# Splitting the halves of exchanged weight blocks over two DMA queues in a lightning-attention and tanh-shrink kernel

## The chip, the cores and the metric

The kernel runs on one core of one Trainium2 chip. The metric is the device time of one execution in microseconds (us), the median of several. A core has five engines that run side by side, each in its own order: TensorE (PE) for matrix products, VectorE (DVE) and ScalarE (ACT) for elementwise work, GpSimd (POOL) and SyncE (SP). Data moves between the chip's memory and the core's buffers by DMA. A DMA is issued as an instruction on SP, ACT or POOL, in that engine's order. The profile shows an engine's issuing as SPq, ACTq or POOLq.

## What is computed

```python
for b in range(nb):                      # blocks of 64 positions, 4 batches, 8 heads of width 64
    sl = slice(b * block, (b + 1) * block)
    qb, kb, vb = (q[:, :, sl], k[:, :, sl], v[:, :, sl])
    intra = np.einsum('bhic,bhjc->bhij', qb, kb) * Dmask[None]
    intra = np.einsum('bhij,bhjd->bhid', intra, vb)
    inter = np.einsum('bhid,bhde->bhie', qb * lam_pow[None], kv_state)
    out[:, :, sl] = intra + inter
    kb_dec = kb * rev_pow[None]
    kv_state = lam_block[None, :, None, None] * kv_state + np.einsum('bhsd,bhse->bhde', kb_dec, vb)
...
x = out.transpose(0, 2, 1, 3).reshape(3072, 512)
h = x @ w_in                             # 512 x 2048
g = h - np.tanh(h)
return g @ w_out                         # 2048 x 512
```

q, k, v are float32 with 4 batches, 8 heads, 768 positions and width 64. The weights w_in and w_out arrive with 64 bits to an element, and the kernel rounds them to float32 itself.

## The kernel before

The sequence is cut into six groups of 128 positions of all four batches (512 rows). Each group passes through the attention and then through the two products with the weights. From the second group on, the products use a Strassen scheme with seven products instead of eight, two levels deep in part. Group 0 is computed plainly, because its time is also the time in which the weights are loaded and rounded: `up_plain` (L740) makes `h`, its tanh and `g`, and `down_plain` (L763) the product with w_out.

The weights come in blocks. `blocks` (L190) lists 16 blocks of w_in, unit u (0 to 3, 512 columns of w_in each) by i (0 to 3, 128 rows each), and then 16 of w_out. This text writes (u,i) for a block of w_in. One block is a tile `raw64` of 128 partitions with 512 numbers of 8 bytes, 512 KB. `load_block` (L195) issues its DMA: for w_out on POOL (L198), for i = 0 and 1 of w_in as one DMA of 128 partitions on SP (L200). For i = 2 and 3, the exchanged blocks, it issues two DMAs of 64 partitions and 256 KB each (L203), one behind the other on SP: the upper and the lower 64 rows change places, because the attention's output has its heads in that order there.

`load_weights(n)` (L205) issues the loads of the first n blocks. There are four `raw64` buffers (`WAHEAD`, L68), so the load of a block waits until the block four places before it has been read. `weights(n)` (L215) rounds the first n blocks, each by `round_block` (L252), and keeps the loads four blocks ahead. Rounding a block is two ACT instructions (`Abs` at L261, here "abs", and a copy of the low words into a buffer `r` at L264, of which there are two), and then four on DVE (L265, L267, L269, L271). L269 and L264 are the last to read the raw block, and L271 finishes the float32 block `w`.

At the start (L277 to L284) SP gets, in this order: q, k, v of batches 0 and 1, q and k of batch 2, blocks (0,0) and (0,1), q and k of batch 3, block (0,2) in two halves, v of batches 2 and 3, and block (0,3) in two halves. Then follow the other blocks. `tied` (L118) keeps the instructions that it is given in the order in which they are written; the loads of w_in are tied. All else may be moved by the scheduler of the framework, which lays down a fixed order for each engine when the program is built. The sequence of group 0 is written out by hand from L784 to L818: attention steps of two batches at a time (`att_transpose`, `att_decay`, `att_scores`, `att_state`, `att_out`), with steps of `up_plain(0, ...)` (the generator `half`) and calls of `weights` between them. `up_plain(u, cs)` goes through the blocks i = 0 to 3 for the output banks `cs`, of which there are four (11, 21, 12, 22), each with eight matmul rows in the profile to a pair of banks and block, or four for one bank. When the last block of a bank is done, ACT takes the tanh (`th`, L757) and DVE subtracts it (`g`, L758).

Of the kernel before, what the change touches and what calls it, by code (L numbers as in the profile page):

```python
# [23 lines left out]
def kernel(  # L24
# [32 lines left out]
    nc = tc.nc  # L57
# [60 lines left out]
    def tied(yes, op):  # L118
        return tc.keep_in_program_order(op) if yes else op
# [69 lines left out]
    w_in_u = moe_w_in.rearrange("k (a n) -> k a n", a=2)  # L189
    blocks = [("in", u, i) for u in range(NU) for i in range(KI)] + [("out", kt, a) for kt in range(KH)  # L190
                                                                    for a in range(2)]
    ready = {"loaded": 0, "done": 0}
    wraw, pair = {}, {}

    def load_block(eng, dst, kind, n, m, first=False):  # L195

        if kind == "out":
            eng.dma_start(out=dst, in_=moe_w_out[ts(m * KH + n, 128), :].rearrange("k (a n) -> k a n", a=2))  # L198
        elif m < 2:
            tied(first, eng.dma_start(out=dst, in_=w_in_u[ts(m, 128), :, ts(n, 256)]))  # L200
        else:
            for j in range(2):
                tied(first, eng.dma_start(out=dst[ts(1 - j, 64)], in_=w_in_u[ts(2 * m + j, 64), :, ts(n, 256)]))  # L203

    def load_weights(n):  # L205

        while ready["loaded"] < min(n, len(blocks)):
            if moe_w_in.dtype != F32:
                raw64 = stage.tile([128, 2, 256], I64, name="raw64", tag="raw64", bufs=WAHEAD)
                block = blocks[ready["loaded"]]  # L210
                load_block(nc.sync if block[0] == "in" else nc.gpsimd, raw64, *block, block[0] == "in")
                wraw[ready["loaded"]] = raw64
            ready["loaded"] += 1

    def weights(n):  # L215

        while ready["done"] < min(n, len(blocks)):
            at_ = ready["done"]
            load_weights(at_ + WAHEAD)
            kind, n_, m = blocks[at_]  # L220
            if kind == "out" and m == 0:
                pair[n_] = wst.tile([128, 8, 256], F32, name="wt", tag="w")
            w = w1[n_][:, m] if kind == "in" else pair[n_][:, 2 * m:2 * m + 2]
            if at_ in wraw:
                round_block(w, wraw.pop(at_), at_ < 2 * KI)
            else:
                load_block(nc.gpsimd, w, kind, n_, m)
            ready["done"] += 1
# [44 lines left out]
    def bank(name, tag, bufs):  # L273
        return psum.tile([128, 512], F32, name=name, tag=tag, bufs=bufs)
# [45 lines left out]
    def att_scores(g, bs):  # L320
        for b in bs:
            qt, kt, _ = tr[g, b]

            sp = [bank("sp", "att", 4).rearrange("s (p i) -> s p i", p=NP) for _ in range(2)]
            for p in range(NP):
                for j in range(2):
                    tied(g == 0, nc.tensor.matmul(out=sp[j][:, p, :], lhsT=kt[ts(j, 64), p, :],  # L327
                                                  rhs=qt[ts(j, 64), p, :], start=True, stop=True))
            ss = work.tile([128, 2, NP, BLK], F32, name="ss", tag="ss")
            for j in range(2):  # L330
                tied(g == 0, nc.vector.tensor_tensor(ss[:, j], sp[j], mask[:, j], op=AL.mult))  # L331
            sc[g, b] = ss
# [26 lines left out]
    def att_out(g, bs):  # L359
        half = bs[0] // 2  # L360
        xt[g, half] = xpool.tile([128, KI, HB], F32, name=f"xt{half}", tag=f"xt{half}")

        ops = [bank("op", "att", 4).rearrange("d (p b s) -> d p b s", p=2, b=2) for _ in range(2)]

        def dst(n, p, j):
            return ops[p // 2][ts(j if p < 2 else 1 - j, 64), p % 2, n, :]


        if g > 0:
            for n, b in enumerate(bs):  # L370
                for p in (0, 1):
                    for j in range(2):
                        r = ts(j, 64)
                        for pp in (p, p + 2):
                            nc.tensor.matmul(out=dst(n, pp, j), lhsT=state[r, b, pp, :], rhs=tr[g, b][2][r, pp, :],  # L375
                                             start=n == 0 and p == 0, stop=False, skip_group_check=True)
        for n, b in enumerate(bs):
            ss, vn = sc.pop((g, b)), raw[g, b]["v"]
            for p in range(NP):
                for j in range(2):  # L380
                    tied(g == 0, nc.tensor.matmul(out=dst(n, p, j), lhsT=vn[:, 2 * p + j, :], rhs=ss[:, j, p, :],  # L381
                                                  start=g == 0 and n == 0 and p % 2 == 0,
                                                  stop=n == 1 and p % 2 == 1, skip_group_check=True))
        for x in range(2):
            tied(g == 0, nc.scalar.activation(
                xt[g, half][:, 2 * x:2 * x + 2, :].rearrange("d p (b s) -> d p b s", b=2), ops[x], AF.Copy))
# [353 lines left out]
    def up_plain(u, cs):  # L740

        hm = {}
        for c in cs:
            a, t = divmod(c - 11, 10)
            hm[c] = bank("h", ("ya", "yb", "z", "w")[2 * t + a], 1).rearrange("q (m c) -> q m c", m=2)
        for i in range(KI):
            for c in cs:
                a, t = divmod(c - 11, 10)
                for m in range(2):
                    tied(u == 0, nc.tensor.matmul(  # L750
                        out=hm[c][:, m, :], lhsT=w1[u][:, i, a, ts(m, 128)], rhs=xt[0, t][:, i, :],
                        start=m == 0 and i == 0, stop=i == KI - 1, skip_group_check=True))
                if (i, c) != (KI - 1, cs[-1]):
                    yield
        for c in cs:
            th = work.tile([128, 2, HB], F32, name="th", tag="th")
            nc.scalar.activation(th, hm[c], AF.Tanh)  # L757
            nc.vector.tensor_tensor(hidden(0, c)[:, u], hm[c], th, op=AL.subtract)  # L758
        yield
# [29 lines left out]
    half = up_plain(0, (11, 21))  # L789
    att_transpose(0, (2,))  # L790
    att_decay(0, 2)
    weights(1)
    att_out(0, (0, 1))
    att_scores(0, (2,))
    next(half)
    weights(2)
# [139 lines left out]
```

## Time and profile before

| | |
|---|---|
| median of 3 runs | 673.6 us |
| lowest, highest | 673.12, 675.31 us |
| the profiled execution | 674.1 us |
| its span, first to last instruction | 672.3 us |
| TensorE clock granted | 1.000 |
| PE rows in the profile | 4824 |
| DMA queue of SP (q1) | 133,536 packets, 31.50 MB |
| DMA queue of POOL (q0) | 28,976 packets, 96.49 MB |

A row of the profile's groups, waits or timeline names the line of the kernel, the engine and the tiles, written as output <- inputs. A wait is put down to what came last by the profile. In the timeline the columns are the start, the time taken, engine and line, the operation, the shapes and the number of instructions that were merged, with the idle time before them in brackets. In the chain of waits the columns are the start, the time taken, and what it was.

The stage that the change lies in is the first 85 us. Its busy times by stretch, with the number of instructions:

```profile
core 0: us, PE busy (x) PEld busy (x) DVE busy (x) ACT busy (x) POOL busy (x), PEclk, DMA share, GB/s
...
15.00:20.00 5.00, 3.98 (x50) 3.26 (x46) 4.09 (x9) 3.48 (x7) 0.00 (x0) 1.00 1.09 236
20.00:25.00 5.00, 4.20 (x32) 3.48 (x32) 3.87 (x7) 2.44 (x4) 0.00 (x0) 1.00 1.04 206
25.00:32.00 7.00, 5.87 (x77) 4.75 (x76) 4.70 (x10) 3.95 (x8) 0.00 (x0) 1.00 0.91 236
32.00:40.00 8.00, 8.00 (x39) 7.04 (x38) 7.59 (x16) 5.75 (x10) 0.00 (x0) 1.00 0.68 203
40.00:50.00 10.00, 10.00 (x48) 8.81 (x47) 9.93 (x20) 6.80 (x13) 0.00 (x0) 1.00 0.75 211
```

In the first three of these stretches PE is idle for part of the time; from 32 us on it is busy throughout. POOL does nothing there. DVE is busy for 9.93 of the 10 us from 40 to 50.

### The profile page before, as it was taken

How to read it: one execution, taken by the hardware profiler on the slowest of the kernel's cores; microseconds unless marked ns; L12 is line 12 of the kernel's file. 1: busy time of each engine (PE TensorE's matmuls, PEld its weight loads, DVE VectorE, ACT ScalarE, POOL GpSimd, SP SyncE). 2: the span in 40 equal slices, each digit the busy share in tenths (PEclk: the TensorE clock that was granted, in tenths of full speed). 3: DMA queues.
4: the chain of work that ended last, by engine and by line, in shares of the span. 5: the costliest groups of instructions: out<-in, count | busy, mean ns of one | idle time of the engine just before them, and what ended most of it. 6: DMA issues, size and time to landing. Idle time of an engine off the chain costs nothing.

```text
span 672.3 us, 12869 instructions
## 1 busy us (share of the span) xinstructions
PE 661.7 (98%) x4824; PEld 576.3 (86%) x4824; DVE 481.3 (72%) x872; ACT 194.8 (29%) x373; POOL 200.5 (30%) x345
## 2 busy tenths in 40 slices
PE   8899999999999999999999999999999999999998
PEld 7688855558888999988999988899988899988997
DVE  4797867993887772499895379888358977357743
ACT  4564433423331111332112243112333112234110
POOL 0001424217332424244345201254300245400351
PEclk9999999999999999999999999999999999999999
DMA  9979799869855978587898632698730677610495
GB/s 209 222 205 236 238 268 255 290 147 271 249 148 139 243 191 210 127 239 236 228 285 253 176 80 58 150 292 255 225 73 13 160 236 220 217 35 1 126 289 164
DMA packets 162717, 128.80 MB, mean 192 GB/s; under 512 B 133856, under 2 KB 135008, under 8 KB 162656
## 3 DMA queue, kind: packets, MB, share of 16 engines
q0 software_dynamic: 28976, 96.49, 45.4%
q1 hardware_dynamic: 133536, 31.50, 23.6%
q8 instruction: 38, 0.62, 0.4%
q14 instruction: 23, 0.19, 0.1%
q10 hardware_dynamic: 144, 0.00, 0.0%
HBM read 103.55 MB, written 24.38 MB: 190 GB/s over the span
## 4 chain that ended last, share of the span: by engine, by line
PE 86%; issue 8%; DMA 2%; SPq 1%; POOL 1%; DVE 0%; ACT 0%; POOLq 0%; DVEq 0%; ACTq 0%
PE y L433 13%; PE y L695 11%; PE op L771 8%; PE z L433 8%; PE zw L695 8%; PE h L750 7%; PE w L642 4%; PE y L642 4%; PE y L517 4%; PE sp L327 3%; PE plain L642 3%; PE op L381 3%; PE z L517 2%; PE op L375 2%; PE kv L349 1%
## 5 line engine op out<-in xcount | busy, mean ns | idle before, releaser
L607 POOL DMA_DIRECT2D wb<-fine x147 | 79.4, 541 | 114.7 <-PE y L695 48.2
L610 POOL DMA_DIRECT2D wb<-factors x56 | 30.3, 543 | 155.2 <-PE y L642 97.3
L441 ACT ACTIVATE th<-g 128x512 f32<-128x512 f32 x76 | 47.6, 630 | 98.3 <-DVE g L446 33.2
L433 PE MATMUL y<-xt,w 128*128 128x256 f32 x320 | 74.0, 380 | 0.0
L433 PEld LDWEIGHTS y<-xt,w 128*128 128x128 f32 x320 | 59.9, 190 | 9.0 <-ACT g L521 0.9
L442 DVE TENSOR_TENSOR g<-g,th 128x512 f32<-128x512 f32 x76 | 51.9, 688 | 18.2 <-ACT th L441 18.1
L698 ACT ACTIVATE q<-y 128x128 f32<-128x128 f32 x84 | 23.3, 278 | 130.1 <-PE y L695 126.5
L750 PE MATMUL h<-xt,w 128*128 128x256 f32 x256 | 56.5, 381 | 2.0 <-DVE w L271 2.0
L771 PE MATMUL op<-wt,g 128*128 128x512 f32 x128 | 56.5, 595 | 0.0
L750 PEld LDWEIGHTS h<-xt,w 128*128 128x128 f32 x256 | 48.2, 190 | 9.2 <-DVE w L271 1.4
L695 PE MATMUL y<-wb,g 128*128 128x128 f32 x384 | 51.2, 278 | 0.0
L771 PEld LDWEIGHTS op<-wt,g 128*128 128x128 f32 x128 | 23.8, 190 | 27.7 <-issue 26.5
L695 PEld LDWEIGHTS y<-wb,g 128*128 128x128 f32 x384 | 46.4, 192 | 1.2 <-issue 0.3
L433 PE MATMUL z<-tt,ws 128*128 128x256 f32 x160 | 38.0, 380 | 0.0
L433 PE MATMUL z<-xt,ws 128*128 128x256 f32 x160 | 37.9, 380 | 0.0
L433 PE MATMUL y<-tt,ws 128*128 128x256 f32 x160 | 37.8, 379 | 0.0
L642 PE MATMUL y<-wb,g 128*128 128x256 f32 x160 | 35.6, 379 | 0.5 <-PE y L433 0.5
L198 POOL DMA_DIRECT2D raw<-in_moe_w_out_dram x16 | 8.9, 555 | 90.8 <-DVE g L758 52.3
L642 PE MATMUL w<-wb,g 128*128 128x256 f32 x160 | 35.8, 382 | 0.0
L331 DVE TENSOR_TENSOR ss<-sp,mask 128x512 f32<-128x512 f32 x48 | 30.9, 682 | 6.0 <-PE sp L327 6.0
L642 PEld LDWEIGHTS y<-wb,g 128*128 128x128 f32 x160 | 30.3, 190 | 5.0 <-PE y L433 0.9
L433 PEld LDWEIGHTS z<-xt,ws 128*128 128x128 f32 x160 | 30.3, 190 | 4.3 <-ACT g L449 0.2
(171 smaller groups left out, 1301.2 us busy)
## 6 DMA issues: line engine op xcount, KB each, us to landing
wb<-fine POOLq DMA_DIRECT2D x147, 256.0 KB, 3.9
wb<-factors POOLq DMA_DIRECT2D x68, 256.0 KB, 4.2
raw<-in_moe_w_out_dram POOLq DMA_DIRECT2D x16, 512.0 KB, 5.2
v_nat<-in_v_dram SPq DMA_DIRECT2D x24, 256.0 KB, 5.4
factors<-wt POOLq DMA_DIRECT2D x8, 768.0 KB, 5.0
wb<-fine_in POOLq DMA_DIRECT2D x24, 256.0 KB, 4.1
k_nat<-in_k_dram SPq DMA_DIRECT2D x20, 256.0 KB, 5.0
raw<-in_moe_w_in_dram SPq DMA_DIRECT2D x8, 512.0 KB, 5.9
```

Of the source, the lines that this page charges most:

```text
L331: tied(g == 0, nc.vector.tensor_tensor(ss[:, j], sp[j], mask[:, j], op=AL.mult))
L433: nc.tensor.matmul(out=t[:, m, :], lhsT=wt[:, kt, ts(m, 128)], rhs=x[:, kt, :], start=first and m == 0 and kt == 0, stop=kt == 1, skip_gro ...
L441: nc.scalar.activation(th, src, AF.Tanh)
L442: nc.vector.tensor_tensor(dst(c), src, th, op=AL.subtract)
L517: nc.tensor.matmul(out=dst[:, ts(u, 128)], lhsT=a, rhs=b, start=x in (1, 2, 5) and u == 0, stop=True, skip_group_check=True)
L607: nc.gpsimd.dma_start(out=t.rearrange("p m c -> p (m c)"), in_=fine[TWICE.index(n_), SUB.index(x_)].rearrange("p u c -> p (u c)"))
L610: nc.gpsimd.dma_start(out=t, in_=factors[XAT[FACT[n_][1]]][:, 2 * x_:2 * x_ + 2, :])
L642: nc.tensor.matmul(out=t[:, m, :], lhsT=a[:, u, kt, ts(m, 128)], rhs=wb[:, kt, :], start=first and u == 0 and m == 0 and kt == 0, stop=u = ...
L695: nc.tensor.matmul(out=dst, lhsT=a[:, u, :], rhs=wb[:, ts(u, 128)], start=x in (1, 2) and u == 0, stop=u == NU - 1, skip_group_check=True)
L698: nc.scalar.activation(keep, dst, AF.Copy)
L750: tied(u == 0, nc.tensor.matmul(out=hm[c][:, m, :], lhsT=w1[u][:, i, a, ts(m, 128)], rhs=xt[0, t][:, i, :], start=m == 0 and i == 0, stop= ...
L771: nc.tensor.matmul(out=obank[b], lhsT=g, rhs=wt[:, 2 * a:2 * a + 2, :], start=kt == 0 and a == 0, stop=kt == KH - 1 and a == 1)
```

## The change

The two DMAs of an exchanged block go to two queues. The lower half of the tile (rows 2m+1, `half(eng, 1, first)`) stays on SP, tied as before. The upper half goes to another queue. For unit 0 its issue is put into a list `deferred`, which is worked off on ACT, tied, after `att_out(0, (0, 1))`. For units 1 to 3 it is issued on POOL, not tied. The w_out blocks and the blocks of i = 0 and 1 are loaded as before.

```diff
     ready = {"loaded": 0, "done": 0}
-    wraw, pair = {}, {}
+    wraw, pair, deferred = {}, {}, []
 
     def load_block(eng, dst, kind, n, m, first=False):
...
         elif m < 2:
             tied(first, eng.dma_start(out=dst, in_=w_in_u[ts(m, 128), :, ts(n, 256)]))
         else:
-            for j in range(2):
-                tied(first, eng.dma_start(out=dst[ts(1 - j, 64)], in_=w_in_u[ts(2 * m + j, 64), :, ts(n, 256)]))
+
+            def half(queue, j, yes):
+                tied(yes, queue.dma_start(out=dst[ts(1 - j, 64)], in_=w_in_u[ts(2 * m + j, 64), :, ts(n, 256)]))
+
+            half(eng, 1, first)
+            if n == 0:
+                deferred.append((half, nc.scalar, 0, True))
+            else:
+                half(nc.gpsimd if first else eng, 0, False)
...
     att_decay(0, 2)
     weights(1)
     att_out(0, (0, 1))
+    for fn, *args in deferred:
+        fn(*args)
     att_scores(0, (2,))
     next(half)
     weights(2)
```

## The prediction

> **What bounds the kernel now.** I read the page's busy table first, then the waits of TensorE (PE), then the chain of work over the first 75 us, and last the timelines of SP, ScalarE (ACT), VectorE (DVE) and PE there, because all that the change touches is issued before 52 us.
>
> ```profile
> PE 661.7 (98%) x4824; PEld 576.3 (86%) x4824; DVE 481.3 (72%) x872; ACT 194.8 (29%) x373; POOL 200.5 (30%) x345
> ...
> PE h L750 <- DVE w L271: 2.0, 2, 1.0
> PE tp L311 <- ACT qt L313: 0.8, 1, 0.8
> PE kv L349 <- DMA v_nat<-in_v_dram: 0.2, 1, 0.2
> ```
>
> PE is busy 98% of the span, so time can be won only in its few idle stretches, while every stall that is added to PE's order comes on top. The waits of PE under 35 us are 1.0 us at 18.44 and 0.96 us at 31.41 (the two of the first line), 0.8 us at 20.80 and 0.2 us at 26.09. The first is block (0,0), loaded before anything that moves. The second ends in this chain:
>
> ```profile
> 13.43 3.06 SPq L203
> ...
> 19.27 2.89 SPq L203
> ...
> 22.20 5.92 DMA raw<-in_moe_w_in_dram
> ...
> 28.20 0.68 ACT w L261
> ...
> 30.66 0.70 DVE w L271
> ...
> 31.41 43.65 PE h L750 x201
> ```
>
> "SPq" is the SP queue busy with issuing: an issue that takes 0.6 us [...] took 3.06 and 2.89 us at the first halves of blocks (0,2) and (0,3). The last half of (0,3) then lands 5.92 us after its issue, at 28.12; ACT and DVE round the block by 31.36, and PE starts on it 0.96 us late. From 31.41 PE runs without a gap to 81.58 and beyond:
>
> ```profile
> 31.41 50.34 PE L750 MATMUL h<-xt,w 128*128 128x256 f32 x232 [0.96 <-DVE w L271]
> ```
>
> That is the cover of units 1 to 3. It is thinnest at block (1,3). One block for one output bank is four rows of this group, 4 x 50.34/232 = 0.868 us. After (0,3) come 2 + 8 such pieces of unit 0 and three of unit 1, so PE reaches (1,3) at 31.41 + 13 x 0.868 = 42.7. DVE finishes it at 40.78 + 0.69 = 41.47, ahead of both `g` subtractions:
>
> ```profile
> 37.80 0.66 ACT L261 ACTIVATE w<-raw 128x512 f32<-128x512 f32 x1
> 39.54 0.60 ACT L757 ACTIVATE th<-h 128x512 f32<-128x512 f32 x1 [1.08 <-PE h L750]
> 40.03 0.68 ACT L264 ACTIVATE r<-raw 128x512 int32<-128x512 uint32 x1
> 40.61 0.59 ACT L757 ACTIVATE th<-h 128x512 f32<-128x512 f32 x1
> 41.42 0.68 ACT L261 ACTIVATE w<-raw 128x512 f32<-128x512 f32 x1 [0.23 <-DMA raw<-in_moe_w_in_dram]
> ...
> 40.78 0.69 DVE L271 CUSTOM_DVE_ANT_0 w<-w,r 128x1024 uint16<-128x1024 uint16 x1
> 41.38 1.28 DVE L758 TENSOR_TENSOR g<-h,th 128x512 f32<-128x512 f32 x2
> ```
>
> The slack of (1,3) is thus 1.2 us; ACT's rows at 37.80 and 41.42 are the blocks (2,0) and (2,1), each taken as it lands.
>
> [...] the halves of (2,3) land at 45.12 and 46.40, 256 KB in 1.28 us (205 GB/s), those of (2,2) 1.08 us apart (243 GB/s), and block (0,1) of 512 KB lands 1.53 us after (0,0) (343 GB/s). [...] The trace shows only ACT's one issue of 4 KB: 0.42 us.
>
> **Part 1, unit 0: two halves leave SP and go to ACT.** SP loses two issues; (0,2) and (0,3) keep their lower halves there. ACT gets two issues behind the `xt` copies, that is at 17.37. At SP's unhindered 0.55 to 0.60 us they take 1.15 us. ACT is idle from 18.48 to 20.08 (1.60 us, waiting for PE's transposes), and DVE takes the one thing behind them, the rounding of (0,1), only at 19.41; delayed by 1.15 us, its `Abs` ends at about 19.1. So the issues are hidden, with 0.45 us to spare. Below nothing isn't possible for ACT; above, the bound is the rival B.
>
> What it gains: [...] v for batches 2 and 3 moves up by one half, and the last half of (0,3) by one half of its own and one of (0,2). Against this ACT's two halves (landing, by SP's 4.8 to 5.5 us, at 22.5 to 23.5) share the engines. If all serialize[...], the sum of bytes before (0,3) is the same and it lands at 28.1, while v for batch 3 lands one half (1.1 us) later, at 27.05: PE's products with it, then `op` and (0,2), end at 31.5, and (0,3) starts where it starts now. Gain 0. If they overlap[...], (0,3) lands up to 1.1 us earlier, and all 0.96 us of the gap goes; what is late next is v (25.95) and PE's own work before it. (0,2) has room either way: rounded at 27.05, used at 28.45. I take 0.4 us.
>
> **Part 2, units 1 to 3: six halves go from SP to POOL.** POOL is idle until 53.61, and waits there for the same slot as SP does. Six issues of 0.53 us cost PE nothing; its w_out loads stay behind them in block order. A load of 512 KB from POOL lands 4.3 to 4.5 us after an issue on a quiet queue, a block from SP 4.8 to 5.2. So pairs land together, about 1 us earlier than now. That is worth nothing, since PE has no gap here.
>
> **Part 3, what moves with it.** PE's order is the same. But the built order of ACT and DVE in unit 1 changes (lines of the kernel before):
>
> ```
> ACT before: abs(1,3) r(1,3) abs(2,0) th  r(2,0) th      abs(2,1)
> ACT after:  abs(1,3) abs(2,0) r(1,3) r(2,0) th abs(2,1) th
> DVE before: L269(1,2) L271(1,2) .. L269(1,3) L265(2,0) L271(1,3) g g
> DVE after:  L265(2,0) L269(1,2) L267(2,0) L271(1,2) .. g L269(1,3) g L271(1,3)
> ```
>
> Rounding (1,2) now stands behind (2,0), and finishing (1,3) behind the second `g`, whose tanh stands behind abs(2,1). Both blocks are still waited for. With the landings of today (37.77 and 41.40; SP issues them when (1,0) and (1,1) are used up, at 32.95 and 36.25, as now) and these rows' durations:
> - by (2,0): abs 37.80, DVE L265 38.52, L269(1,2) 38.85, L267 39.45, L271(1,2) 39.79 to 40.48; it frees the `r` buffer, so r(2,0) 40.53, th 41.10, abs(2,1) 41.60, th 42.18, g 42.81, L271(1,3) 43.41 to 44.10.
> - by (2,1): landed 41.40, abs 41.42, th 42.0, g 42.6, L271(1,3) 43.2 to 43.9.
> So PE reaches (1,3) at 44.15, not 42.7: 1.4 us lost. [...] it rises by each us that they land later. Behind it (2,3) has 4.5 us of slack, (3,2) and (3,3) 4.4 and 3.7; their new orders use up 2 to 3 us, so nothing more is lost. After 85 us the orders agree.
>
> **Sum.** The stall is 1.4, the start gives 0.4 back and shifts everything with it: +1.0 us. The profiled execution took 674.1 us (span 672.3 and 1.8 around it), 0.5 over the median of 673.6. So 675.1 on its scale and 674.6 on the median's, +0.15%. A measurement tells about 0.3%, 2.0 us, from no change.
>
> **The cases.**
> - A, the forecast, 0.60: 674.6, own range 673.6 to 675.4 (gain 0.96 and stall 1.0, to gain 0 and stall 1.8).
> - B, slower, 0.15: ACT's issues are held up. [...] they wait while SP pushes v [...], and take SP's 1.43 to 3.06 us each. For: SP's issues in just that stretch[...]. Place: ACT's `qt` of batch 3 at 20.08. Two issues are 2.9 to 6.1 us; less 1.6 of idle time and the 0.96 at 31.41, 0.3 to 3.5 are lost, in the middle 1.9. With the stall of 1.4: +3.3, 676.9. It decides from some 1.6 us an issue.
> - C, 0.15: the second queue slows the blocks that (1,3) now waits for. One block of unit 3 took 6.11 us to land; at that, (2,1) lands at 42.36 and (1,3) starts at 44.9, +2.2 with no gain at the start: 675.8, the edge of what can be told.
> - D, 0.10: the blocks land early enough that the new order costs nothing, and the whole gap goes: -1.0, 672.6. The 0.8 us at 20.80 (k for batch 3, landed 20.66, issued before anything moves) would have to go too for -1.8.
> That the change does nothing is A with both terms near 0. Faster by over 0.3% needs more idle time than the touched stretch has: 0.05. Slower gets most of B, two thirds of C and a little of A: 0.29. Within: 0.66. The range 672.8 to 677.0 leaves out part of B.
>
> **What would show it.** Right: the gap before PE's (0,3) shrinks from 0.96; a new PE wait `h L750 <- DVE w L271` of 1 to 2 us near 43; ACT's issues take under 0.7 us each and `qt` stays near 20.1; no new PE gap from 45 to 85. Wrong: no wait near 43, ACT's `qt` past 20.5, v for batch 3 after 27, or gaps after 100 us that differ from today's.

## The result and the profile after

The changed kernel takes 677.06 us (22 runs, 674.47 to 679.62) beside 673.59 us of the kernel before in the same comparison (22 runs, 672.21 to 675.31). The ratio is 1.0049 with an interval of 1.0038 to 1.0060: slower by 2.6 to 4.0 us, where +1.0 had been forecast. The profiled execution took 677.29 us (span 675.5), 3.2 more than that of the kernel before. From `load_weights` on, the lines of the changed kernel stand 8 lower down in the file than those of the kernel before.

Waits of PE over the whole span (who waited for what: total us, times, longest):

```profile
PE h L758 <- DVE w L279: 2.8, 3, 1.4
PE kv L357 <- DMA v_nat<-in_v_dram: 1.9, 1, 1.9
...
PE z L441 <- DVE g L472: 0.9, 1, 0.9
PE y L703 <- DMA wb<-fine: 0.8, 1, 0.8
```

The first two are those of before, one more in number and much longer for `v_nat` (it was 0.2). The third is new. PE's busy time is the same (662.0 us, it was 661.7), so nearly all of the loss is waiting. Its timeline shows where:

```profile
20.00 0.60 PE L319 MATMUL tp<-ident,k_nat 128*128 128x128 f32 x4
...
27.00 0.69 PE L357 MATMUL kv<-v_nat,k_nat 128*64 128x64 f32 x16 [1.90 <-DMA v_nat<-in_v_dram]
...
32.02 11.49 PE L758 MATMUL h<-xt,w 128*128 128x256 f32 x52 [0.66 <-DVE w L279]
44.24 2.00 PE L758 MATMUL h<-xt,w 128*128 128x256 f32 x8 [0.74 <-DVE w L279]
...
179.34 2.00 PE L441 MATMUL z<-xt,ws 128*128 128x256 f32 x8 [0.89 <-DVE g L472]
```

Put instruction by instruction beside the trace of before, PE's lateness grows in these steps: the transposes at 20.80 came 0.80 us earlier, v's products at 26.09 came 0.91 late, block (0,3) is 0.61 late (32.02 for 31.41), block (1,3) 1.51 (44.24 for 42.73), the product `z` 2.67 (179.34 for 176.67), and the end about 3.2. That is +0.6 at the start, +0.9 at (1,3), +1.2 near 179 us, and about +0.5 in single waits for `wb<-fine` after 440 us, net of one of 0.96 us that only the kernel before had (at 643.95).

The step at (1,3) is the one that had been worked out, as DVE's timeline shows:

```profile
41.70 0.69 DVE L766 TENSOR_TENSOR g<-h,th 128x512 f32<-128x512 f32 x1
42.31 0.68 DVE L277 SCALAR_TENSOR_TENSOR w<-raw,w 128x512 uint32<-128x512 uint32 x1
42.91 0.68 DVE L766 TENSOR_TENSOR g<-h,th 128x512 f32<-128x512 f32 x1
43.51 1.28 DVE L279 CUSTOM_DVE_ANT_0 w<-w,r 128x1024 uint16<-128x1024 uint16 x2
```

The finishing operation of (1,3) (L279) starts at 43.51, behind both `g`; PE starts at 44.24. The forecast had 43.41 and 44.15. The block itself wasn't late: its second half had landed at 36.54, and ACT was done with it at 38.99.

ACT's and SP's timelines at the start:

```profile
16.18 0.69 ACTq L205 DMA_DIRECT2D raw<-in_moe_w_in_dram  x1
...
16.90 1.64 ACTq L205 DMA_DIRECT2D raw<-in_moe_w_in_dram  x1
...
18.59 0.68 ACT L269 ACTIVATE w<-raw 128x512 f32<-128x512 f32 x1 [1.05 <-issue]
...
20.26 0.60 ACT L321 ACTIVATE qt<-tp 128x512 f32<-128x512 f32 x1 [0.42 <-PE tp L319]
```

```profile
13.20 3.28 SPq L205 DMA_DIRECT2D raw<-in_moe_w_in_dram  x1
16.54 2.08 SPq L130 DMA_DIRECT2D v_nat<-in_v_dram  x2
18.66 2.55 SPq L205 DMA_DIRECT2D raw<-in_moe_w_in_dram  x1
```

ACT's second issue took 1.64 us while SP was issuing v (2.08 us from 16.54), yet the idle time behind it hid this: `qt` starts at 20.26, 0.18 later than before. SP, with one half less to issue ahead of v, still took 3.28 and 2.55 us for the halves that it kept. What counts is the order of the landings: SP's half of (0,2) at 20.46, ACT's 22.23, v of batch 2 at 23.79, ACT's half of (0,3) 25.46, v of batch 3 at 26.87 (before 25.95), SP's half of (0,3) 28.71 (before 28.12). 256 KB land every 1.4 to 1.8 us, the first five alternately from SP's and from ACT's queue. So not only v is late. From the landing of k for batch 3 to that of the last half of (0,3), these six transfers took 9.4 us, and 7.5 before. PE's last wait ahead of (0,3), 0.66 us at 32.02, is for that block.

### The profile page after: what moved, and what is told of

Same layout as the page of the kernel before. It is cut to its first block, busy times and chain, and to the rows that moved or that the text cites. A ratio compares the mean times of both kernels' runs of the same rounds, so it can differ in the third digit from the quotient of the medians.

```text
span 675.5 us, 12875 instructions
## 1 busy us (share of the span) xinstructions
PE 662.0 (98%) x4824; PEld 577.1 (85%) x4824; DVE 481.5 (71%) x872; ACT 194.8 (29%) x373; POOL 203.7 (30%) x351
## 4 chain that ended last, share of the span: by engine, by line
PE 74%; issue 9%; DMA 7%; DVE 4%; POOL 2%; SPq 2%; ACT 1%; POOLq 0%; DVEq 0%; ACTq 0%
PE y L441 11%; PE y L703 10%; PE z L441 7%; PE zw L703 7%; PE h L758 6%; PE op L779 5%; PE w L650 4%; PE y L650 4%; PE y L525 4%; PE plain L650 3%; DMA raw<-in_moe_w_in_dram 3%; PE sp L335 3%; PE op L389 2%; PE z L525 2%; SPq L142 2%
## 5 line engine op out<-in xcount | busy, mean ns | idle before, releaser
L650 PEld LDWEIGHTS w<-wb,g 128*128 128x128 f32 x160 | 30.1, 190 | 4.3
```

Source lines behind the costliest of these rows:

```text
L650: nc.tensor.matmul(out=t[:, m, :], lhsT=a[:, u, kt, ts(m, 128)], rhs=wb[:, kt, :], start=first and u == 0 and m == 0 and kt == 0, stop=u = ...
```

## The experiments

Two explanations of the steps after 85 us stood against each other. T1: PE, late by 1.5 us, meets a crowded stretch of DMAs worse than before. T2: the six POOL transfers change something fixed in POOL's later stream. Every kernel was timed in turn with the kernel before on the same chip, 5 to 22 times, and the ratios are to that. The last four columns are from the one profiled execution: PE's start at (0,3), its wait at (1,3), POOL's idle time ahead of a transfer near 151 us, and PE's wait at `z`, a product of a later group, near 178 us. The transfer carries sums of w_out blocks (pair kt 7) to `factors`, a buffer in the chip's memory; the recorded texts call it the factors load. Lines stand 9 lower than in the kernel before in e1, e2, e9 and e12, 8 in e8, 12 in e10 and 13 in e11.

| kernel | median us | ratio, interval | (0,3) | (1,3) | POOL | near 178 |
|---|---|---|---|---|---|---|
| before | 673.6 | 1 | 31.41 | none | 9.31 | none |
| changed | 677.06 | 1.0049 (1.0038 to 1.0060) | 32.02 | 0.74 | 10.36 | 0.89 |
| e1 ACT alone | 675.46 | 1.0038 (1.0025 to 1.0051) | 31.93 | none | 9.32 | none |
| e2 POOL alone | 675.57 | 1.0041 (1.0027 to 1.0054) | 30.79 | 1.07 | 10.36 | 0.85 |
| e3 six small | 676.28 | 1.0039 (1.0027 to 1.0050) | 31.45 | none | 10.36 | 0.77 |
| e4 PE late | 675.63 | 1.0031 (1.0019 to 1.0043) | 30.45 | none | 9.31 | none |
| e5 unchanged | 673.71 | 1.0007 (1.0000 to 1.0013) | 30.53 | none | 9.32 | none |
| e6 memsets | 674.38 | 1.0021 (1.0013 to 1.0029) | 31.09 | none | 9.32 | none |
| e7 eight small | 675.66 | 1.0030 (1.0020 to 1.0040) | 31.19 | none | 9.30 | none |
| e8 tied | 679.73 | 1.0089 (1.0071 to 1.0107) | 34.06 | none | 10.36 | 1.08 |
| e9 units 2, 3 | 674.21 | 1.0015 (1.0006 to 1.0024) | 31.23 | none | 10.31 | 0.47 |
| e10 changed + two | 676.12 | 1.0037 (1.0025 to 1.0049) | 31.49 | 0.78 | 9.30 | none |
| e11 e9 + four | 674.62 | 1.0020 (1.0013 to 1.0028) | 31.67 | none | 9.30 | 0.24 |
| e12 ACT late | 678.03 | 1.0068 (1.0054 to 1.0081) | 35.84 | none | 9.32 | none |

**The parts alone (e1, e2), as changes to the changed kernel.**

```diff
# e1: n == 0 as in the changed kernel, else both on SP
-                half(nc.gpsimd if first else eng, 0, False)
+                half(eng, 0, first)
...
# e2: n == 0 both on SP, else as in the changed kernel
-                deferred.append((half, nc.scalar, 0, True))
+                half(eng, 0, first)
```

> Unit 0's two lower halves on ScalarE, the blocks of units 1 to 3 both halves on SP as before. What stands in the trace of the changed kernel for the start is k for batch 3 earlier (-0.8 us at 20.8) and v for batch 3 late (+0.9 at 27.0, +0.5 behind it): net +0.6 us at block (0,3). Prediction's part 1 alone: -0.4, 673.2 us. T1 (early stalls, enlarged later only because PE is later): start +0.6 with no stall at (1,3), so 674.2 to 674.8. T2 (six POOL transfers change later waits whatever PE's time): no POOL transfers here, so +0.6, 674.2, and the waits of the stretch 145 to 180 us stay as before. A gain of 0.5 us or more would say that the start of the changed kernel is slow because of something in units 1 to 3.

> Unit 0 on SP alone as before, six halves of units 1 to 3 on POOL. Both theories: the start as before (gap of 0.96 us at (0,3) and 0.8 at 20.8 are there), and a stall at (1,3) of 1.0 to 1.5 us near 43.5. T1: then enlarged later by less than in the changed kernel, since PE is 1.0 to 1.5 us late instead of 1.5 at 45 us: +1.2 to +2.2, 674.8 to 675.8 us. T2: the stall plus the full later loss of about 1.7 us that the changed kernel shows after 85 us: +2.9, 676.5 us, and PE's gap near 179 us is there.

(The "lower halves" of the e1 text are the upper halves of the tile in the words of this document.) PE's timeline of e1 has the wait for v and no other up to 80 us; its tail near 178 us is clean:

```profile
27.45 0.69 PE L358 MATMUL kv<-v_nat,k_nat 128*64 128x64 f32 x16 [1.70 <-DMA v_nat<-in_v_dram]
```

That of e2 has the start of before and the stall at (1,3):

```profile
30.79 11.49 PE L759 MATMUL h<-xt,w 128*128 128x256 f32 x52 [1.12 <-DVE w L280]
43.35 16.89 PE L759 MATMUL h<-xt,w 128*128 128x256 f32 x77 [1.07 <-DVE w L280]
```

So the late v belongs to ACT's part; the stall and the wait near 178 belong to POOL's. The median of e1 is about 1 us above what was expected and what its profile shows; that profiled run, 674.43 us, was the lowest of its five. The median of e2, 675.57, lies in the range of T1 and 0.9 under the figure of T2; but the wait near 178 us, which T2 asks for, is there.

**POOL's stream, or PE's lateness (e3, e4, as changes to the kernel before).** e3 leaves all loads as they were and adds six transfers of 512 bytes, so that POOL's later transfers have the semaphores that they have in the changed kernel. (In the trace of the kernel before, the 339 transfers of POOL carry eight semaphores, numbers 111 to 118, in turn and without a break, and so do the 345 in that of the changed kernel. The transfer to `factors` near 151 us is the 42nd and has 112 in the first; it is the 48th and has 118 in the second.) e4 leaves POOL alone and makes PE late.

```diff
# e3, ahead of the attention of group 0
+    for n in range(6):
+        nc.gpsimd.dma_start(out=extra[:, n:n + 1], in_=ident[:, n:n + 1])
...
# e4, ahead of down_plain; the products are not used
+    for _ in range(7):
+        tc.keep_in_program_order(nc.tensor.matmul(out=wait[:, 0:128], lhsT=ident, rhs=ident, start=True, stop=True))
```

> The kernel before with six small transfers (512 bytes each) on POOL's queue at its start and nothing else changed, so that each later POOL transfer gets another of POOL's semaphores, as in the changed kernel. T1: no PE stall before 85 us, so no loss after it: 673.6 us (within 0.3). T2: the loss after 85 us appears without any early stall: +1.2 to +2.0, 674.8 to 675.6 us, with a PE gap near 179 us and POOL's factors load of kt 7 late near 153 us.

> The kernel before with seven extra 128x128 products on PE at 81.6 us (about 7 x 0.22 = 1.55 us, the delay that the changed kernel has there), nothing else changed; their result is not used. T1: what follows is late as in the changed kernel, so the later loss of 1.7 us comes too: +3.0 to +3.4, 676.6 to 677.0 us, with a PE gap near 179 us. T2: only the added work itself, +1.5 us, 675.1 us, and no new gap near 179 us.

T1 falls, by PE's timeline of e4. The added products put `op` at 82.19 (80.71 in e5, below: +1.48), and no wait near 178 us follows (nor one in e12, where PE is over 5 us late from 42 us on):

```profile
80.62 1.73 PE L825 MATMUL wait<-ident 128*128 128x128 f32 x14
82.19 7.03 PE L771 MATMUL op<-wt,g 128*128 128x512 f32 x16
```

In e3 nothing is late at 85 us, and yet the wait is there. Neither median is the one that T2 expected: e4 is 0.5 us above it, e3 0.7 above its range, and the profiled execution of e3 (675.50) was the fastest of its five. POOL's timeline, of before and then of e3, shows the root. The transfer to `factors` needs the last subtraction of `sums_out` (L243), which DVE ended at 150.66 in the one and 150.71 in the other:

```profile
150.96 0.84 POOL L246 DMA_DIRECT2D factors<-wt  x1 [9.31 <-DVE wt L243]
152.41 0.58 POOL L776 DMA_DIRECT2D out_dram<-ob  x1 [0.61 <-issue]
```

```profile
152.06 0.84 POOL L246 DMA_DIRECT2D factors<-wt  x1 [10.36 <-DVE ws L235]
152.89 0.56 POOL L776 DMA_DIRECT2D out_dram<-ob  x1
```

POOL takes it 0.30 us after its input in the first, and 1.35 us after in the second. The `ws` named as releaser is only the DVE instruction that ended last: the transfer carries `wt`, and in the traces of the kernel before and of the changed kernel it waits on the same semaphore of DVE (107). From here the delay is handed on. The following lines are DVE's timeline near 175 us, before and then e3, and PE's of e3:

```profile
174.81 0.69 DVE L590 TENSOR_TENSOR wt<-wq,wt 128x512 f32<-128x512 f32 x1 [0.21 <-DMA fine<-wt]
```

```profile
176.31 0.69 DVE L590 TENSOR_TENSOR wt<-wq,wt 128x512 f32<-128x512 f32 x1 [1.66 <-DMA fine<-wt]
176.92 0.68 DVE L464 TENSOR_TENSOR g<-g,z 128x512 f32<-128x512 f32 x1
```

```profile
177.66 1.99 PE L433 MATMUL z<-xt,ws 128*128 128x256 f32 x8 [0.77 <-DVE g L464]
```

The later transfer to `factors` lets POOL write `fine` later (first at 154.05 before, 154.52 in e3, 156.08 in the changed kernel) and so read `wq` back later (162.91 before, 164.35 in e3, 165.79 in the changed kernel). DVE then waits for the transfer that frees its `wt`, with the `g` that PE needs standing behind in DVE's order.

**Which property of POOL's stream (e5, e6, e7).** Six more transfers turn the semaphores of all later ones by six of the eight, add six to their count, and shift every instruction by nine places (e3) or fifteen (changed kernel: the transfer to `factors` has 102 instructions of POOL ahead of it in the trace, 87 before). e6 shifts by nine places without a transfer (`nc.gpsimd.memset` of nine columns); e7 is e3 with `range(8)`: count and place move, the turn is whole. e5 is the kernel before, unchanged.

> The kernel before, unchanged, as a control: how much of the +0.3 to +0.4% of the four variants so far is in the comparison itself, and what a second profile of the same program shows. If the comparison is even: 673.3 us, ratio 1.000. If a variant comes out higher only because it is a second program: about 674.5, ratio 1.002. In the profile: k for batch 3 at 20.7 us and v at 26.0 again if the start always goes as in the first profile, other times if the 0.8 us at 20.80 are chance; the gap near 179 us stays away in every theory.

> The kernel before with nine one-column memsets on POOL at its start, so that POOL's later instructions stand nine places on in its stream, as they do with the six small transfers, but with the same number of transfers and the same semaphores. L (semaphores of transfers, or their count): POOL takes the factors load of kt 7 at 151.0 us, no PE gap near 179, 673.3 us. P (place in POOL's instruction stream): POOL takes it about 1.0 us later (152.0), PE has a gap of about 0.8 us near 178, +1.0 or more: 674.3 to 676.3 us.

> The kernel before with eight small transfers on POOL at its start: each later transfer has the semaphore that it has in the kernel before, and stands thirteen places on in POOL's stream, eight transfers on in its count. L as the turn of semaphores: factors load of kt 7 at 151.0 us, no PE gap near 179 us, 673.3 us. L as the count of transfers, or P (place in the stream): at about 152.0, gap near 178 us, 674.3 to 676.3 us. Together with the nine memsets the two are told apart.

POOL's wait is 9.32 and 9.30 us in e6 and e7, and PE has no wait near 178 in either, so neither place nor count alone makes it. Both times missed the 673.3 that went with this. In e7 PE was 1.3 us later than in e5 at 12.5 us: 0.4 from the first loads, which landed later, the rest in a stretch (8.42 to 11.83) in which the granted clock was 0.50. At (0,3) 0.7 of it were left, and the +2 us of the median aren't in its profile, whose execution (673.53) was the lowest of its runs. In e6 PE waits 0.97 us for `wb<-factors` at 303.7.

The control gave more than an even comparison. Its profiled execution has a span of 670.1 us, 2.2 less than the first one of the same program. PE's timeline at the start:

```profile
19.88 0.63 PE L311 MATMUL tp<-ident,k_nat 128*128 128x128 f32 x4
...
30.53 29.84 PE L750 MATMUL h<-xt,w 128*128 128x256 f32 x137 [0.99 <-DVE w L271]
```

The 0.8 us at 20.80 and the 0.96 us at 643.95 of the first profile aren't there. They are chance, and so is the earlier k of the changed kernel.

**The order in unit 1 (e8, e9).** e8 is the changed kernel with the rounding of units 0 and 1 and of the next two blocks, and the tanh and `g` of unit 0, all tied, so that (1,3) is finished ahead of the two `g`. e9 is e2 with unit 1 back on SP too, which gives ACT and DVE their old order there.

```diff
# e8
-                round_block(w, wraw.pop(at_), at_ < 2 * KI)
+                round_block(w, wraw.pop(at_), at_ < 2 * KI + 2)
+        # L267, L269, L271 of round_block tied when first; th and g of up_plain tied for u == 0
...
# e9
-            if n == 0:
+            if n < 2:
                 half(eng, 0, first)
                 half(eng, 1, first)
```

> The changed kernel with unit 1's rounding kept in order, so that block (1,3) is finished ahead of the two g. If the stall at (1,3) comes from the order of DVE alone: the gap of 0.74 us at 44 us goes, PE's delay stays at the +0.6 us of the start until 170 us, and about 0.9 us come back: 676.1 us. If it comes from blocks (2,0) and (2,1) landing late on two queues: the gap stays at about 0.7 us and the time at 677. The later loss near 179 us stays in both, since the POOL transfers are all there.

> Units 0 and 1 both halves on SP, units 2 and 3 on SP and POOL: four POOL transfers instead of six, and ScalarE and DVE take unit 1 in the order of the kernel before. If the stall at (1,3) comes from the order in unit 1: PE has no gap between (0,3) and 80 us, and reaches (1,3) 11.3 us after (0,3), as in the kernel before (12.2 and 12.6 with the new order). If it came from POOL's queue as such, a gap of 0.7 to 1.2 us would appear at (2,3) or later. POOL's semaphores are turned by four, not six: if any turn other than eight holds the factors load of kt 7, it has the wait of 10.36 us and PE the gap near 178 (674.3 to 675 us); if six alone does, 9.3 us, no gap, and 673.3.

e8 answers nothing. v landed at 28.11 in it, PE waited 2.84 us for it, and the granted clock then was 0.50 for 3.41 us, so that PE was 2 us later than in the changed kernel and would hardly have stalled at (1,3) in any order. Its order moved a stall of 2.01 us to the last block of unit 3, at 75.09. e9 does answer. First PE's timeline, then DVE's:

```profile
31.23 28.97 PE L759 MATMUL h<-xt,w 128*128 128x256 f32 x133 [1.11 <-DVE w L280]
```

```profile
40.61 0.69 DVE L280 CUSTOM_DVE_ANT_0 w<-w,r 128x1024 uint16<-128x1024 uint16 x1
41.21 1.28 DVE L767 TENSOR_TENSOR g<-h,th 128x512 f32<-128x512 f32 x2
```

DVE finishes (1,3) ahead of both `g`, and PE runs from 31.23 through units 1 to 3 without a wait, with POOL still loading for units 2 and 3. So the stall belongs to the order in unit 1, not to a second queue as such. (e9 also brings unit 1's halves back to SP; but in the changed kernel (1,3) had landed 7 us before its last operation began.) With a turn of four, POOL's wait is 10.31 us: six isn't special. In e9 the wait ends 0.04 us before the second `ws` of DVE does, in the other four 0.01 to 0.02 us after it. By these times the end of `ws` can't be what ended it in e9; but they are close, and what holds the transfer stays open.

**The turn put right (e10, e11).** Two small transfers behind the last POOL half of unit 3 in the changed kernel, four in e9, make the turn eight.

```diff
+                if first and (n, m) == (3, 3):
+                    for x in range(2):      # 4 in e11
+                        tied(True, nc.gpsimd.dma_start(out=extra[:, x:x + 1], in_=ident[:, x:x + 1]))
```

> The changed kernel with two more small POOL transfers right after its last half of unit 3, so that from there on each POOL transfer has the semaphore of the kernel before. If the later loss is the turn of the semaphores: the factors load of kt 7 waits 9.3 us instead of 10.36, PE's gap of 0.89 us near 179 goes, about 1.2 us come back: 675.9 us, the gaps at 27, 32 and 44 us stay. If it is the six transfers as such: nothing changes, 677.1.

> Units 2 and 3 on SP and POOL, units 0 and 1 on SP, and four small POOL transfers behind them, so that the semaphores are those of the kernel before: each of the three places where the changed kernel loses time is taken out. If these three are the whole loss: 673.3 us, ratio 0.999 to 1.001, no PE gap at 27, 44 or 178 us beyond those of the kernel before. If the second queue costs something of its own: 674 or more. A gain over the kernel before is not expected, since PE doesn't wait for units 2 and 3.

POOL's timeline of e10, then DVE's:

```profile
152.09 0.83 POOL L258 DMA_DIRECT2D factors<-wt  x1 [9.30 <-DVE wt L255]
```

```profile
176.07 0.69 DVE L602 TENSOR_TENSOR wt<-wq,wt 128x512 f32<-128x512 f32 x1
```

POOL's wait is that of before, DVE doesn't wait for `fine<-wt`, PE's wait near 178 is gone, and the median, 676.12, is near the 675.9 expected (its interval overlaps that of the changed kernel, so the traces carry this step). So for this transfer the turn decides, as far as turns were tried: held in all kernels with a turn of four or six (changed, e2, e3, e8, e9), not held in the nine whose turn is whole. e11 missed. It is still slower by 0.1 to 0.3%, and its profile isn't free of the three places: with unit 0 on SP alone PE still waits 1.29 us for v (landed at 26.14, 0.2 later than before; PE had come early), and 0.24 us near 178, with POOL's wait at 9.30. PE's timeline has a further reason, a wait that was 0.53 us (for PE's own `y`) in e5:

```profile
26.27 0.69 PE L362 MATMUL kv<-v_nat,k_nat 128*64 128x64 f32 x16 [1.29 <-DMA v_nat<-in_v_dram]
...
305.15 0.67 PE L655 MATMUL y<-wb,g 128*128 128x256 f32 x2 [1.30 <-DMA wb<-factors]
```

In e6, e10 and e11 POOL's transfers of 291 to 294 us run beside SP's loads of k and v for the next group, the first of which come 3 to 5 us later there than in e5, and land late. That isn't shown to be the cause: in e2 they come as late (286.6, in e5 282.75), and PE has no such wait. What sets it was not tried.

**Why v is late (e12).** As e1, with ACT's issues behind its copies of batch 3's transposes.

```diff
     att_transpose(0, (3,))
+    for fn, *args in deferred:
+        fn(*args)
```

> ScalarE's two halves of unit 0 issued behind its copies of batch 3's transposes, about 5 us later than with unit 0 alone on ScalarE; units 1 to 3 on SP. If v for batch 3 is late because ScalarE's halves go through the DMA engines ahead of it: v lands at 25.1 us or before, PE's gap of 1.7 us at 27.4 goes, and the halves become late instead: block (0,2), needed at 28 to 29 us, is finished at 30 or after, and PE reaches (0,3) at 31.5 to 33 us; 675.0 to 676.5. If v is late because SP's issues are slower beside a second queue: v stays at 26.9 to 27.4 us.

PE's timeline, then ACT's:

```profile
24.73 1.15 PE L358 MATMUL kv<-v_nat,k_nat 128*64 128x64 f32 x32
25.71 1.92 PE L390 MATMUL op<-ss,v_nat 128*64 128x128 f32 x32
32.26 28.10 PE L759 MATMUL h<-xt,w 128*128 128x256 f32 x116 [4.63 <-DVE w L280]
```

```profile
21.03 1.48 ACTq L205 DMA_DIRECT2D raw<-in_moe_w_in_dram  x2
29.07 0.66 ACT L270 ACTIVATE w<-raw 128x512 f32<-128x512 f32 x1 [7.46 <-DMA raw<-in_moe_w_in_dram]
```

v lands at 23.87 and doesn't hold PE. The halves, 8.0 and 9.5 us on their way beside SP's next blocks, land at 29.05 and 31.16, and PE waits 4.63 us at (0,2). The landings are as the first of the two cases expected: with ACT's halves issued ahead of v it is v that lands late, with ACT's halves issued later it is they. Over all kernels, v for batch 3 lands at 25.04 to 26.14 with unit 0 on SP (nine kernels), at 26.87 to 28.11 with ACT's early issues (four), and at 23.87 here. The price is 1.5 us above the top of the range, and (0,3) came at 35.84 in place of 31.5 to 33. A part of it is the clock. In these stretches of e12, of which the first lies in PE's wait, the third number from the end is the granted clock:

```profile
28.00:32.00 4.00, 0.00 (x0) 0.00 (x0) 2.04 (x4) 2.46 (x5) 0.00 (x0) 0.89 0.54 123
32.00:38.00 6.00, 5.74 (x14) 4.58 (x15) 4.84 (x10) 3.89 (x8) 0.00 (x0) 0.50 0.62 188
38.00:42.00 4.00, 4.00 (x20) 3.54 (x19) 3.58 (x7) 2.91 (x6) 0.00 (x0) 1.00 0.35 113
```

From 31.13 to 37.96 the granted clock was 0.50, and PE's rows stand 0.43 us apart in place of 0.22. In e8 the same came with a wait of 2.84 us; with waits of up to 2.01 us (e8 at 75.09) it didn't. ACT's two issues here took 0.74 us each, beside issues of SP of 0.56 us.

No version tried beats the kernel before.

## Why the prediction was right in part and wrong in size

Forecast were 674.6 us and a range to 677.0; measured were 677.06, at its upper edge (the ratio of 1.0049 on the forecast's 673.6 gives 676.9). The sign was right, a third of the size was there. That the range nearly holds the result is luck: its upper end was there for case B, which isn't what happened.

- **Part 3, the stall at (1,3): right.** Forecast 1.4 us with PE at 44.15; measured 44.24, with the order, the wait and its releaser as worked out. The part of it that is the change's own is 0.9 us in the changed kernel and 1.2 in e2 (43.35 less 30.79 is 12.56, 11.33 of it work). The forecast stall was larger because it let PE come to (1,3) at 42.7; PE came 0.6 us later, which takes as much off the stall.
- **Part 1, "I take 0.4 us": wrong in sign.** The serial case had v at 27.05; it landed at 26.87 and 27.32 (e1). The step that failed is "the sum of bytes before (0,3) is the same and it lands at 28.1", with PE at (0,3) "where it starts now", 31.41. The last half landed at 28.71 and 28.63, and PE was at 32.02 and 31.93. The 31.41 was itself late by chance. The nine kernels with unit 0 on SP have 30.45 to 31.67, mean 31.1; the changed kernel, e1 and e10 have 32.02, 31.93 and 31.49, mean 31.8 (e8, with its halved clock, 34.06). So the part costs about 0.7 us where 0.4 was to be gained, by one profile of each kernel. From k to the last half of (0,3) the six transfers took 8.2 to 9.4 us with ACT's early issues (four kernels), and 7.3 to 7.7 on SP alone (eight of nine; 8.9 in e11): two queues were no faster, and mostly slower. Why was not tried. ACT's two halves landed in between SP's transfers (22.23 between 20.46 and 23.79, 25.46 between 23.79 and 26.87). The overlap for which the forecast allowed up to 1.1 us was its author's estimate, and didn't come.
- **"The issues are hidden": right.** They took 2.3 us in place of 1.15 and pushed `qt` by 0.18 us. Case B's price per issue (decides from 1.6 us) was met by one of two (1.64 us; the other took 0.69), and its place wasn't: the total near its 676.9 is no support for it. What makes an issue take 1.4 us and more there is not shown.
- **Part 2: right.** From the first issue to the last landing the exchanged blocks of units 2 and 3 took 4.6 to 6.1 us, 5.6 to 6.6 before, about 0.7 us less in place of 1; (1,2), beside the traffic of the start, took 9.1 for 7.3. No wait of PE changed by it.
- **"so nothing more is lost. After 85 us the orders agree": the other step that failed.** The orders do agree. The turn of POOL's semaphores doesn't (112 before, 118 after for the transfer to `factors`), and it costs 1.2 us near 179 us in the profile. The forecast had named the sign of it ("gaps after 100 us that differ from today's") and no price.
- **Case C: wrong.** (2,1) landed at 40.99, not at 42.36.

With +0.7 at the start, +0.9 at (1,3) and +1.2 near 179 us the sum is +2.8 us, beside 2.6 to 4.0 measured. That doesn't close the account. e11, without ACT's issues, the new order and the turn, is still 0.9 to 1.9 us slower than the kernel before, and e6, which moves no transfer, 0.9 to 2.0. In e1, e3 and e7 the median is 0.8 to 2.1 us above the profiled execution, which was the fastest of each. So the three steps are shown in the traces, but not that they are all of the loss; how much any small change of this program costs is not known. Waits for `wb` loads after 300 us differ by about 1 us between kernels, and between the two profiles of the unchanged one.

## What to carry to other kernels

A second queue added no room here, where the DMA engines were busy for 0.9 to 1.1 of the stretches from 15 to 32 us (the six transfers up to (0,3) took 9.4 us in place of 7.5): it changed who lands first. So ask which load a moved one overtakes and who waits for that one. A moved issue also moves what a scheduler places afterwards, and it moves the turn of the semaphores of every later transfer on that queue (here by six of eight, with POOL 1.35 us after its input in place of 0.30); a control that changes only these (small transfers, then as many as make the turn whole) tells such a cost from that of the change. Take a second profile of the unchanged kernel before pricing gaps of under 1 us, and look at the granted clock behind every new long wait of PE (it was 0.50 behind those of 2.84 and 4.63 us here).

## What was not expected of the hardware

- POOL took a transfer 1.3 to 1.35 us after its input in five kernels (turn of four or six) and 0.3 us after in the nine others (turn of none or eight), with the same instruction, which waits on the same semaphore of DVE (107) in the traces of the kernel before and of the changed one. No row shows what holds it.
- The kernel with six more transfers of 512 bytes took 0.27 to 0.50% longer (e3), that with nine memsets on an idle POOL 0.13 to 0.29% (e6); no wait of PE in the profile of e6 is over 0.5 us longer than in e5.
- In e8 and e12 the granted clock fell to 0.50 some 3.5 us after PE had stopped, for 3.41 and 6.83 us, and so also over the first rows after the wait. e1 and e7 have such a stretch of 3.41 us too, from 7.80 and 8.42, with no PE wait of over 0.7 us shortly ahead.
- Two executions of one program differed by 2.2 us of span, through two waits of 0.8 and 0.96 us at loads.
